# Another load order for the first units and a newly chosen order of all operations in a fused gated-linear-attention and GELU-FFN kernel

## The chip, the cores and the metric

The kernel runs on one core of one Trainium2 chip. The metric is the device time of one execution in microseconds (us); lower is better. The core has a matrix engine (TensorE; in the profile PE, its weight loads PEld), VectorE (DVE), ScalarE (ACT), GpSimd (POOL), and SyncE (SP), which here only issues transfers. Sixteen DMA engines move data between the chip's memory (HBM) and the core's working memory (SBUF); matrix products land in eight banks of PSUM.

## What is computed

The reference is a gated linear attention followed by a feed-forward block, both without biases:

```
B, H, S, D = 4, 8, 768, 48
f = sigmoid(f_logit)
for t in range(S):                       # per batch and head, state is D x D
    state = f[t][:, None] * state + outer(k[t], v[t])
    y[t]  = q[t] @ state
x = y reordered to (B*S, H*D)            # 3072 tokens x 384
h = x @ w_in                             # 384 x 2048
out = gelu_exact(h) @ w_out              # 2048 x 384
```

Inputs and the output are float32; the kernel multiplies in bfloat16 and accumulates in float32.

## The kernel before

**Tiling.** The 3072 tokens are cut into 24 chunks of 128 tokens, n = 0 to 23, and two chunks make a unit, u = 0 to 11 (chunks 2u and 2u+1; three units are one batch entry). Instead of stepping the recurrence token by token, each chunk is done with matrix products: decays are cumulated in the log domain, queries and keys are scaled by them, scores inside the chunk are masked, and a 48 x 48 state per head is carried from chunk to chunk. Each unit is also one group g of the feed-forward block.

**Names of the operations.** The names below are those in the code; a number after them is the chunk n or the unit u.

| name | engine | what it is (line) |
|---|---|---|
| fl, kt, vt, qt | SP queue | loads of logits, k, v, q of a unit: one of 384 KB for units 0 to 4 (L513), two of 192 KB from unit 5 on (L521) |
| i0, i1, i2; o0 to o3 | POOL queue | w_in in three pieces, 1024 + 512 + 512 columns (L525); w_out in four (L528) |
| E, L | ACT | exp and ln of a unit's logits (L558, L561), 0.84 us each |
| C | PE | cumulative log decays (L590, L591, L585) |
| RG, GT, GL | ACT | exp of them, both signs, and of the chunk's total (L607, L613, L634) |
| KP, QP | DVE or POOL | k and q times their decays, into tile sc (L640) |
| VC | POOL or ACT | v cast to bfloat16, into tile vb (L647) |
| Tk, Tq, then KQ | PE, then DVE or ACT | transposes of sc (L876) and their copy from PSUM (L884), units 0 to 3 |
| KD | SP queue | the same transposes done by DMA, from unit 4 on (L864) |
| A, AM | PE, DVE | scores (L1058, L995) and their masking (L901) |
| S, R, T, SB | PE, DVE, POOL, POOL | the chunk's part of the state (L1085, L1093, L1018), its addition, its decay, its copy in bfloat16 (L730, L735, L738; L925, L927, L932) |
| YI, YX, Y, YB | PE, DVE or ACT | outputs from the scores (L1113), from the state (L975), both together (L1031), and their copy (L945) |
| XT, X; XD | PE, DVE or ACT; SP queue | transposes of y (L961, L964); by DMA from unit 5 on (L949) |
| F1.g.u, GE | PE, ACT | h = x w_in in 8 parts per group (L1165, 6 matmuls, about 0.65 us) and GELU (L1175) |
| F2.n.r, O, st | PE, DVE or ACT, SP queue | out = gelu(h) w_out in four parts r per chunk, part r needing w_out piece r (L1186), its copy (L1191), its store (L1200) |

**What sets the order.** Every operation is first recorded with its engine, its reads and writes, its buffers and an assumed duration. `Plan.run` then places all of them one by one in the sequence that the list `ORDER` gives (the numbers are places in the recording order), gives each a planned start and a buffer, and the program is emitted by planned start. Each engine executes its own instructions strictly in the emitted order, so an instruction that waits holds back everything behind it on that engine. The planner's times are used for nothing else, with one exception: before a PE operation that opens a PSUM bank in the first `WARM` = 30 us, the planner fills the planned gap with multiplications of a zero tile `junk` (L1241).

**Loads.** `LOADS` fixes the order of the input transfers. On SP they are only queued, eight semaphores in turn, so the ninth load is issued when the first has landed. Where the kind of queue changes, `load` adds a wait on an earlier transfer (`gate`): i0 waits for the fourth load before it, i1 for f2, f3 for o3. The waiting instruction sits in the issuing engine's own order:

```
if order[j][0] != eng and ahead >= (AHEAD if eng == "pool" else 1.4):
    gate = late if late is not None and ahead > 5.3 and eng == "pool" else order[j][1]
```

**Tables and banks.** exp/ln and GELU are in different ACT tables, so a change between them costs a table load (L1247). The eight PSUM banks are four for F1, F2 and a few named units (`s_fh`) and four for the rest.

**Lists that choose engines.** `HVC` (units whose VC is on ACT), `HKQ` (chunks whose KQ is on ACT), `HYB`, `HX` (chunks whose YB, X is on ACT), `GKP`, `GQP` (chunks whose KP, QP is on POOL), `EG`, `ET` (units whose C or Tk/Tq use the F1 banks), `AJ` (units whose two score products are one operation).

Of the kernel before, what the change touches and what calls it, by code (L numbers as in the profile page):

```python
# [191 lines left out]
RST = []  # L192
VA = []
WIN = [1024, 512, 512]
EG = [0, 1, 4]
ET = [1]
EX = [0]
EA = [0, 1]
SPLIT = []
HVC = [1, 4]  # L200
HKQ = [0, 1, 2, 6, 8]
HYB = [1, 5]
HX = []
GKP = [2, 8]
GQP = [2, 3, 21]
GAM = []
ODVE = [0, 1, 2, 4, 6, 7, 8, 9, 10, 11, 12, 13, 14, 16, 17, 18, 19, 20, 21, 22, 23]
XDMA = [5, 6, 7, 8, 9, 10, 11]
KDMA = [4, 5, 6, 7, 8, 9, 10, 11]
AJ = [2, 4, 5, 7, 8, 10, 11]  # L210
NGT = 4
NG1 = 3
GLD = []
# [6 lines left out]
AHEAD = 4.4  # L220
UNITS = 12
WARM = 30.0
LOADS = ['f0', 'k0', 'v0', 'q0', 'v1', 'f1', 'k1', 'q1', 'i0', 'f2', 'k2', 'q2', 'v2', 'i1', 'i2', 'o0', 'o1', 'o3', 'o2', 'f3', 'f4', 'k3', 'q3', 'v4', 'q4', 'v3', 'k4', 'f5', 'k5', 'v5', 'q5', 'u6', 'u7', 'u8', 'u9', 'u10', 'u11']

PRIO = []
ORDER = [int(x) for x in """
5 6 0 21 23 22 10 26 18 9 31 20 13 12 27 28 24 7 29 14 32 33 16 15 25 11 17 121 122 123 129 8 124 30 126 130 131 132
125 135 128 34 2 3 4 133 139 136 35 39 134 140 148 127 137 141 36 138 37 38 145 192 193 194 149 152 147 146 19 150 142
151 206 195 197 196 200 201 198 144 143 202 40 41 204 205 156 157 207 210 208 158 153 211 199 203 161 209 219 212 159
160 216 220 221 162 163 223 218 42 43 213 214 265 266 164 166 170 222 215 217 44 154 155 45 47 171 228 167 229 49 230  # L230
267 224 231 232 46 234 235 168 169 233 236 239 240 243 48 50 241 244 237 242 174 245 238 165 172 247 246 173 248 225
279 227 51 53 249 52 178 251 175 250 176 273 253 179 252 177 55 272 259 180 54 56 274 277 269 271 268 270 254 186 260
276 275 283 181 187 278 57 280 284 281 291 58 59 285 292 188 282 189 226 293 295 286 190 331 255 294 332 256 60 61 182
287 288 290 289 401 62 333 339 334 183 296 184 336 335 337 402 340 261 262 341 342 300 297 343 344 347 263 346 298 301
302 299 348 403 404 405 409 63 411 412 410 64 350 349 351 1 345 338 315 305 257 352 355 65 306 66 307 309 354 356 353
414 67 68 358 408 313 359 413 316 308 406 361 362 363 360 69 314 407 317 311 303 415 258 70 310 304 318 312 357 423
417 366 424 367 325 326 370 368 371 372 327 416 467 369 425 328 426 365 468 329 71 185 72 428 429 427 475 364 379 380
373 418 383 73 74 375 381 419 422 374 384 421 420 469 377 376 378 387 476 432 388 75 436 76 264 382 77 481 430 431 78
433 79 389 319 385 437 470 471 478 477 480 472 527 80 81 82 320 434 435 473 474 528 321 438 386 479 322 323 489 390
391 482 441 442 447 443 448 451 483 444 490 445 452 453 439 491 493 535 83 446 454 440 395 484 449 450 455 485 487 84  # L240
492 601 191 85 86 486 488 529 531 530 542 396 536 494 495 496 87 539 537 497 88 89 330 461 397 392 593 456 533 534 540
594 538 541 393 498 462 551 602 604 595 607 457 543 532 597 598 596 603 605 458 557 463 398 503 544 459 606 552 399
558 600 504 90 513 514 559 553 91 561 608 499 464 545 548 505 501 599 550 616 554 560 500 547 549 610 546 617 502 507
508 618 506 562 619 511 623 609 92 93 512 555 509 521 556 563 624 510 625 522 394 94 400 324 564 95 659 667 627 515
611 620 615 613 614 660 516 523 517 518 661 662 663 668 628 96 670 664 669 97 465 612 629 519 621 575 576 98 622 672
524 525 99 577 565 579 569 578 566 665 666 671 573 681 570 580 630 682 567 571 673 100 674 675 641 568 574 683 727 626
685 643 637 572 642 101 644 631 632 102 645 635 646 638 633 676 636 634 639 653 640 103 104 105 654 684 581 680 679
734 106 677 678 107 688 686 108 647 719 655 582 720 721 728 687 689 109 723 724 730 733 722 583 526 520 460 690 725
726 729 732 785 731 648 649 587 588 650 786 656 584 736 743 787 794 651 585 744 795 797 788 735 749 750 589 590 796
791 746 745 793 751 699 790 789 591 110 111 700 740 741 737 742 701 705 754 112 702 586 113 808 693 739 738 747 706  # L250
694 691 692 799 809 755 810 800 748 697 698 695 792 798 592 114 696 707 703 756 704 657 708 709 815 710 802 801 765
769 770 711 816 757 759 760 763 115 116 117 803 771 758 766 764 806 817 118 807 805 761 772 652 658 767 752 753 812
811 859 762 804 768 851 713 820 779 773 774 813 714 821 814 119 712 852 860 862 780 853 775 861 864 822 863 855 858
854 867 856 776 715 781 782 857 783 716 866 873 835 836 717 827 874 777 819 875 818 825 823 826 828 877 120 865 876
718 824 868 872 871 870 833 831 845 829 869 832 880 881 878 837 879 834 830 846 838 847 839 784 848 840 778 882 849
841 842 889 843 890 883 897 884 893 885 894 898 886 887 895 888 891 844 850 466 899 900 896 892 901 902 905 906 903
907 908 911 912 913 909 914 904 915 910 916
""".split()]


# [1 line left out]
def kernel(  # L262
# [268 lines left out]
    def decays(u):  # L531
# [33 lines left out]
        last = 2 * u + 1 if rc[2 * u + 1] % nC == nC - 1 else None  # L565
        gps = [(s_fh if u in EG else s_m).new() for _ in range(1 if g1d else 2)]
        if g1d:
# [83 lines left out]
    def decays_hs(u):  # L651
# [3 lines left out]
        for j in range(2):  # L655
# [9 lines left out]
            def lv(j=j):  # L665
# [4 lines left out]
                  rd=[("e", n)] + z_lf, wr=[("lf", n)], bufs=[fl, lf], table="exp", prio=pr, name=f"L{n}")  # L670
            g = (s_fh if u in EG else s_m).new()

# [70 lines left out]
    def attn_hs(u):  # L743
        kq = s_kq.new()
        for c in range(2):
            n = 2 * u + c
            sc = X[n]["sc"]
            tp = (s_fh if u in ET else s_m).new()
            pr = 20 * u + 10 * c
# [107 lines left out]
    def turn(u, kq):  # L857


        for j in range(2):  # L860
            n = 2 * u + j
            sc = X[n]["sc"]
            if u in KDMA:
# [3 lines left out]
                continue  # L867
            tp = (s_fh if u in ET else s_m).new()
            pr = 20 * u + 10 * j
# [358 lines left out]

    P.run()
    PLAN.append(P)  # L1230
    state = {}
    junk = one.tile([C, 512], BF16, name="junk")
    nc.gpsimd.memset(junk, 0.0)  # L1233
    at = 0.9
    for o in P.placed:
        if o.eng == "PE":
            if o.opens is not None and o.start < WARM:
                room = int((o.start - at - 0.25) / (0.11 if o.start < 10 else 0.06))
                while room > 0:
                    w = 128 * min(room, 4)  # L1240
                    nc.tensor.matmul(o.opens.t()[:, 0:w], junk[:, 0:C], junk[:, 0:w], start=True, stop=True, skip_group_check=True)  # L1241
                    room -= 4
            at = o.end
        if o.table and state.get("t") != o.table:
            state["t"] = o.table
            if o.dur:
                nc.scalar.preload_act_table_set({"exp": "natural_log_exp_and_others", "gelu": "gelu_and_others"}[o.table])  # L1247
        o.fn()
# [32 lines left out]
```

## Time and profile before

| what | value |
|---|---|
| median of 3 runs | 181.52 us (181.39 to 181.66) |
| the profiled execution's own time | 181.36 us, of which its span is 179.6 us |
| PE busy | 170.4 us, 95% of the span, 1996 matmuls |
| ACT busy | 125.9 us (70%), 15 table loads of 1.28 us |
| DVE busy | 94.2 us (52%) |
| POOL busy | 51.9 us (29%) |
| DMA | 32.61 MB, mean 182 GB/s; reads 25.17 MB, writes 4.72 MB |
| granted PE clock | 1.00 throughout |

A line of a timeline reads: start, duration, engine, line of the program, operation, output<-input, shape, count, and in brackets how long the engine sat idle before it and what ended that idle time. A duration of a matmul is its latency; in a row of them the next starts earlier, so busy time, not the sum of durations, is what counts. The chain of waits follows the work that ended last back to its start. The window view gives the busy time of each engine in a stretch.

### The profile page before, as it was taken

Reading aid. Unit: us, or ns where it says so; the run is one execution under the profiler, and the core shown is the slowest. Engines: PE = TensorE matmul, PEld = TensorE weight load, DVE = VectorE, ACT = ScalarE, POOL = GpSimd, SP = SyncE. Lnnn points to the kernel's source line nnn. Section 1 sums busy time; section 2 is a strip of 40 time slices with the busy share of each in tenths; the row PEclk is TensorE's granted clock in tenths of the full one; section 3 lists DMA queues with packets and bytes.
Section 4 is the critical chain, followed back from the end, with each engine's and each line's share of the span. In section 5 each row is a group of like instructions: output and inputs, shape, how many; then the busy total and the mean of one; then the engine's idle time right before and its main releaser. Section 6 shows DMA issues by size and latency. Waiting matters only on the chain.

```text
span 179.6 us, 4905 instructions
## 1 busy us (share of the span) xinstructions
PE 170.4 (95%) x1996; PEld 131.6 (73%) x1998; DVE 94.2 (52%) x195; ACT 125.9 (70%) x214; POOL 51.9 (29%) x117
## 2 busy tenths in 40 slices
PE   7878899999998999999999999999999999999993
PEld 2345679866687787787689599966687976896972
DVE  6347670049887552708688681254892355471110
ACT  3768579955789999988766698677565598351620
POOL 7465684003044540122054414010431410310000
PEclk9999999999999999999999999999999999999999
DMA  6999999989999999789989998898998996932302
GB/s 149 261 261 227 264 165 191 211 199 266 230 193 206 171 232 204 153 186 218 201 159 205 214 208 173 171 182 223 154 246 98 196 241 71 183 86 47 131 0 88
DMA packets 106997, 32.61 MB, mean 182 GB/s; under 512 B 102112, under 2 KB 106080, under 8 KB 106976
## 3 DMA queue, kind: packets, MB, share of 16 engines
q1 hardware_dynamic: 105056, 29.07, 80.7%
q0 software_dynamic: 1776, 3.15, 9.9%
q8 instruction: 15, 0.25, 0.6%
q10 hardware_dynamic: 144, 0.10, 0.2%
q14 instruction: 6, 0.05, 0.1%
HBM read 25.17 MB, written 4.72 MB: 166 GB/s over the span
## 4 chain that ended last, share of the span: by engine, by line
PE 73%; ACT 12%; DVE 5%; DMA 3%; POOL 3%; issue 2%; SPq 1%; POOLq 0%; DVEq 0%; ACTq 0%
PE ps L1186 31%; PE ps L1165 29%; DMA vt<-in_v_dram 3%; ACT gT L1175 3%; DVE am L901 3%; PE ps L995 2%; ACT L1247 2%; POOL sc L640 2%; ACT kq L884 2%; PE ps L1031 2%; PE ps L1211 1%; PE ps L585 1%; ACT rg L607 1%; PE ps L876 1%; PE ps L969 1%
## 5 line engine op out<-in xcount | busy, mean ns | idle before, releaser
L1175 ACT ACTIVATE gT<-ps 128x512 bf16<-128x512 f32 x96 | 57.0, 666 | 24.2 <-PE ps L1165 23.5
L1165 PE MATMUL ps<-xT,win 128*128 128x256 bf16 x576 | 68.8, 273 | 0.8 <-ACT gT L1175 0.5
L1186 PE MATMUL ps<-wout,gT 128*128 128x384 bf16 x368 | 65.9, 326 | 0.0
L1165 PEld LDWEIGHTS <-win 128*128 128x128 bf16 x576 | 61.6, 114 | 3.4 <-issue 0.9
L1186 PEld LDWEIGHTS <-gT 128*128 128x128 bf16 x368 | 34.5, 98 | 19.6
L901 DVE TENSOR_TENSOR am<-ps,mask 128x512 bf16<-128x512 f32 x28 | 17.5, 682 | 17.9 <-PE ps L995 17.9
L927 POOL TENSOR_TENSOR tn<-rr,gl 128x384 f32<-128x384 f32 x12 | 10.3, 857 | 46.0 <-DVE rr L925 45.2
L640 DVE TENSOR_TENSOR sc<-kt,rg 128x384 bf16<-128x384 f32 x22 | 14.6, 668 | 14.4 <-ACT rg L607 14.4
L1191 DVE COPY osb<-ps 128x384 f32<-128x384 f32 x20 | 11.1, 554 | 19.3 <-PE ps L1186 19.2
L1247 ACT ACT_TABLE_LOAD x15 | 19.2, 1283 | 0.3
L647 POOL CAST vb<-vt 128x384 bf16<-128x384 f32 x20 | 10.9, 556 | 24.2 <-DMA vt<-in_v_dram 23.9
L945 DVE CAST yb<-ps 128x384 bf16<-128x384 f32 x22 | 11.5, 552 | 9.6 <-PE ps L1031 5.9
L607 ACT ACTIVATE rg<-ps 128x384 f32<-128x384 f32 x21 | 10.1, 501 | 8.0 <-PE ps L587 2.9
L640 DVE TENSOR_TENSOR sc<-qt,gt 128x384 bf16<-128x384 f32 x21 | 11.6, 558 | 6.0 <-ACT gt L613 5.8
L932 POOL CAST sb<-tn 48x192 bf16<-48x192 f32 x30 | 10.7, 361 | 13.7 <-DVE tn L921 12.6
L558 ACT ACTIVATE fl<-fl 128x768 f32<-128x768 f32 x12 | 10.2, 848 | 6.3 <-DMA fl<-in_f_logit_dram 6.3
L901 DVE TENSOR_TENSOR am<-ps,maskp 128x512 bf16<-128x512 f32 x20 | 12.6, 683 | 3.7 <-PE ps L1061 1.9
L613 ACT ACTIVATE gt<-ps 128x384 f32<-128x384 f32 x21 | 9.9, 493 | 4.0 <-PE ps L587 2.1
L561 ACT ACTIVATE lf<-fl 128x768 bf16<-128x768 f32 x12 | 10.1, 843 | 0.3
L1241 PE MATMUL ps<-junk 128*128 128x512 bf16 (+2 forms) x26 | 8.8, 475 | 1.4 <-POOL junk L1233 1.3
L925 DVE TENSOR_TENSOR rr<-ps,tn 128x384 f32<-128x384 f32 x12 | 6.6, 550 | 2.8 <-PE ps L1018 1.4
L876 PE MATMUL ps<-ident,sc 128*128 128x128 bf16 x64 | 5.1, 219 | 2.1 <-POOL ident masks.py:199 1.5
(84 smaller groups left out, 140.8 us busy)
## 6 DMA issues: line engine op xcount, KB each, us to landing
out_dram<-osb SPq DMA_DIRECT2D x19, 192.0 KB, 3.5
fl<-in_f_logit_dram SPq DMA_DIRECT2D x14, 192.0 KB, 3.9
kt<-in_k_dram SPq DMA_DIRECT2D x14, 192.0 KB, 4.0
vt<-in_v_dram SPq DMA_DIRECT2D x14, 192.0 KB, 3.9
qt<-in_q_dram SPq DMA_DIRECT2D x14, 192.0 KB, 3.9
fl<-in_f_logit_dram SPq DMA_DIRECT2D x5, 384.0 KB, 5.3
kt<-in_k_dram SPq DMA_DIRECT2D x5, 384.0 KB, 6.2
vt<-in_v_dram SPq DMA_DIRECT2D x5, 384.0 KB, 6.2
```

The lines of the kernel that those rows point to most:

```text
L607: P.add("ACT", 0.40, lambda g=gps[j], rg=rg: nc.scalar.activation(rg.t(), g.t()[:, 0:HD], AF.Exp, scale=-1.0), rd=[("g", n)], wr=[("rg", n ...
L640: P.add("POOL" if pl else "DVE", 0.80 if pl else 0.475, lambda a=a, y=y, j=j, w=w, pl=pl, b=(gtv if w else rg): (nc.gpsimd if pl else nc.v ...
L647: P.add("ACT" if hv else "POOL", 0.40 if hv else 0.47, lambda y=y, j=j, hv=hv: (nc.scalar.copy if hv else nc.gpsimd.tensor_copy)(y["vb"].t ...
L901: P.add("POOL" if pl else "DVE", 1.15 if pl else 0.61, lambda hh=hh, pl=pl: (nc.gpsimd if pl else nc.vector).tensor_tensor(ams[hh].t(), ap ...
L927: P.add("POOL", 0.83, lambda: nc.gpsimd.tensor_tensor(tn.t(), rr.t(), glb(), ALU.mult), rd=[("rr", n), ("gl", n)], wr=[("tn", n)], bufs=[r ...
L932: P.add("POOL", 0.36, lambda hh=hh: nc.gpsimd.tensor_copy(sb.t()[64 * hh:64 * hh + D, :, D * hh:D * hh + D], tn.t()[64 * hh:64 * hh + D, : ...
L945: P.add("ACT" if help_ else "DVE", 0.40 if help_ else 0.475, lambda: copier(help_)(yb.t()[:, i, :], yp.t()[:, 0:HD]), rd=[("yp", n)], wr=[ ...
L1165: nc.tensor.matmul(hps.t()[:, i * tok:(i + 1) * tok].rearrange("a (s t) -> a s t", s=s), col(fo)[:, kk, :], xT.t()[:, :, kk, :], start=(kk ...
L1175: nc.scalar.activation(to, fr, AF.Gelu)
L1186: nc.tensor.matmul(op.t()[:, 0:d_model], gT.t()[:, fo, s_ * C:(s_ + 1) * C], wout[fo // 4][:, fo % 4, :], start=(fo == 0), stop=(fo == FO ...
L1191: P.add("DVE" if od else "ACT", 0.475 if od else 0.40, lambda op=op, osb=osb, od=od: copier(not od)(osb.t(), op.t()[:, 0:d_model]), rd=[(" ...
L1247: nc.scalar.preload_act_table_set({"exp": "natural_log_exp_and_others", "gelu": "gelu_and_others"}[o.table])
```

## The change

`LOADS` is changed: f1 comes second instead of sixth, kt0 third, qt0 fourth, vt0 fifth, then qt1, kt1; i0 comes after seven loads instead of eight; vt1 comes behind i0 instead of fifth; vt2 and qt2 change places, vt3 and qt4 too, kt5 comes before fl5, and units 6 and 7 are listed load by load in the order f, k, v, q. The fourth load is now qt0, so i0 waits for qt0 and not for vt1.

`ORDER` is a new list. The lists that choose engines change as shown. Where the emission of junk multiplications looked only at whether an operation opens a bank, it now also looks whether that bank's buffer has been written before (`begun`): in the new order Tq comes before Tk for chunks 0, 2 and 3, and a junk product put ahead of such a Tk would overwrite Tq's result.

```
-EG = [0, 1, 4]
-ET = [1]
+EG = [0, 4]
+ET = [1, 4]
...
-HVC = [1, 4]
-HKQ = [0, 1, 2, 6, 8]
-HYB = [1, 5]
-HX = []
-GKP = [2, 8]
-GQP = [2, 3, 21]
+HVC = [4]
+HKQ = [1, 2, 4, 8]
+HYB = [1, 5, 22]
+HX = [0, 3]
+GKP = [2, 4, 8, 16, 23]
+GQP = [2, 3, 19, 21]
...
-AJ = [2, 4, 5, 7, 8, 10, 11]
+AJ = [2, 4, 5, 7, 10, 11]
...
-LOADS = ['f0', 'k0', 'v0', 'q0', 'v1', 'f1', 'k1', 'q1', 'i0', 'f2', 'k2', 'q2', 'v2', 'i1', 'i2', 'o0', 'o1', 'o3', 'o2', 'f3', 'f4', 'k3', 'q3', 'v4', 'q4', 'v3', 'k4', 'f5', 'k5', 'v5', 'q5', 'u6', 'u7', 'u8', 'u9', 'u10', 'u11']
+LOADS = ['f0', 'f1', 'k0', 'q0', 'v0', 'q1', 'k1', 'i0', 'v1', 'f2', 'k2', 'v2', 'q2', 'i1', 'i2', 'o0', 'o1', 'o3', 'o2', 'f3', 'f4', 'k3', 'q3', 'v4', 'v3', 'q4', 'k4', 'k5', 'f5', 'v5', 'q5', 'f6', 'k6', 'v6', 'q6', 'f7', 'k7', 'v7', 'q7', 'u8', 'u9', 'u10', 'u11']
...
-    state = {}
+    state, begun = {}, set()
...
-            if o.opens is not None and o.start < WARM:
+            if o.opens is not None and o.start < WARM and o.opens not in begun:
...
             at = o.end
+            begun.update(o.bufs)
```

What the new order does to each engine's own sequence in the first part (memsets left out; PE has 23 junk products instead of 28):

```
POOL before: trip, maskp, VC1 VC0, ident, mask, negcol, i0, SB0 SB0, KP2 QP2 QP3, T1 T2, SB.., i1 i2 o0, T3, VC5, SB3, o1 o3 o2, VC4, SB3, T4 ..
POOL after:  negcol, ident, maskp, trip, i0, VC0 VC1, QP2 QP3 KP2, SB0 SB0, T1, SB1 SB1, VC2 VC3, i1, T2, SB2 SB2, i2, mask, VC5, T3, o0 o1 o3 o2, VC4, KP4, T4 ..
ACT before:  E0 L0 RG0 RG1 GT1 GL1 GT0 KQ1 KQ0 E1 L1 VC3 RG2 GT2 RG3 GT3 VC2 GL3 YB1 KQ2 E2 L2 [gelu] 16 GE [exp] RG5 GT4 RG4 GL5 GT5 E3 L3 E4 RG6 GT6 L4 RG7 GT7 GL7 YB5 O3 KQ6 RG8 GT8 GT9 GL9 RG9 [gelu] GE2..
ACT after:   E0 L0 E1 GT0 RG1 GT1 L1 RG0 GT2 KQ1 GL3 RG3 GL1 GT3 RG2 KQ2 YB1 X0 E2 L2 [gelu] GE0.0 X3 15 GE [exp] RG4 RG5 GT4 GT5 GL5 KQ4 E3 L3 E4 L4 RG7 RG6 YB5 GT7 GL9 O3 VC9 GT6 GT8 GL7 GT9 RG8 RG9 [gelu] GE2..
DVE before:  KP0 KP1 QP1 QP0 R0 R1 AM0.1 AM0.1 AM0.0 AM0.0 KP3 YB0 KQ3 X0 R2 X1 AM1 x4 R3 YB2 YB3 X2 X3 ..
DVE after:   KP1 QP0 QP1 KP0 KQ0 AM0.0 AM0.0 AM0.1 AM0.1 KP3 R0 KQ3 YB0 R1 X1 AM1 x4 R2 R3 YB2 YB3 G5 X2 ..
PE before:   C0 C1 Tk1 Tk0 Tq1 S0 Tq0 A0.1 C2 A0.0 C3 YI0 YX1 Tk2 Tk3 Tq2 Tq3 S1 XT0 A1.1 XT1 A1.0 F1.0 x3 YI1 YX2 YX3 C4 XT2 XT3 F1 x13, F2 ..
PE after:    C0 C1 Tk1 C2 Tq0 Tq1 C3 Tk0 A0.0 Tq2 A0.1 Tq3 S0 Tk2 Tk3 YI0 YX1 A1.1 XT0 XT1 A1.0 F1.0 x2, S1, F1.0, YI1 YX2 YX3 C4 XT2 XT3 F1 x13, F2 ..
```

In the later units the sequence of each stage stays the same and single operations change places by a few positions.

## The prediction

> **What bounds the kernel now.** I read the busy tenths of the page first, then the window view, the chain of waits, and last the timelines and waits of the first 60 us engine by engine.
>
> ```profile
> PE   7878899999998999999999999999999999999993
> ```
>
> ```profile
> 21.10:34.20 13.10, 12.88 (x154) 12.14 (x154) 4.79 (x10) 11.93 (x18) 7.19 (x15) 1.00 1.09 193
> 34.20:45.00 10.80, 10.80 (x121) 6.89 (x120) 6.37 (x12) 6.73 (x12) 1.62 (x5) 1.00 1.05 229
> 45.00:54.00 9.00, 8.54 (x153) 6.78 (x153) 7.37 (x16) 7.33 (x15) 1.96 (x3) 1.00 0.96 212
> 54.00:65.40 11.40, 10.76 (x171) 8.87 (x171) 7.49 (x16) 11.30 (x17) 6.40 (x13) 1.00 1.17 199
> 65.40:90.00 24.60, 24.57 (x278) 18.75 (x278) 12.52 (x26) 22.31 (x40) 2.93 (x6) 1.00 0.99 194
> ```
>
> The columns after the stretch are length, then busy time of PE, PEld, DVE, ACT, POOL, the granted clock, DMA share, GB/s. From 21.1 us on PE is the bound: it idles 0.22 + 0 + 0.46 + 0.64 + 0.03 us here, then 0 to 130 us and 0.33 us to 176.7 us, 1.7 us in all. The last 2.9 us are the final copy and store, which stay. Products that count do not change. So the change gains only by (a) bringing the stream that begins with the first F1 forward, and (b) part of those 1.7 us; every new wait behind it costs in full.
>
> ```profile
> 1.86 5.50 DMA vt<-in_v_dram
> ...
> 15.37 3.31 POOL sc L640 x3
> ```
>
> ```profile
> 21.11 2.13 PE L1165 MATMUL ps<-xT,win 128*128 128x256 bf16 x18 [0.17 <-DVE xT L964]
> 21.00 0.85 ACT L558 ACTIVATE fl<-fl 128x768 f32<-128x768 f32 x1 [1.78 <-DMA fl<-in_f_logit_dram]
> 26.48 8.98 ACT L1175 ACTIVATE gT<-ps 128x512 bf16<-128x512 f32 x14 [1.11 <-PE ps L1165]
> 40.72 0.84 ACT L558 ACTIVATE fl<-fl 128x768 f32<-128x768 f32 x1 [2.18 <-DMA fl<-in_f_logit_dram]
> ```
>
> First two pieces of the chain (start, length), then timeline lines of PE and ACT. The lead-in goes by transfers: the trace has the eight first loads landing at 4.33, 5.85, 7.36, 8.86, 10.37, 11.88, 13.38, 14.87 us, one per 1.5 us, i0 at 20.67, fl2 at 20.97 (E2 starts then), the o pieces o0, o1, o3, o2 at 32.73, 34.47, 36.32, 38.18, and fl3, gated by o3, at 40.69 (E3).
>
> **Part 1, to the first F1.** fl1 now lands second, 5.85 instead of 11.88. After L0 (ends 6.07), E1 runs 6.1 to 6.9, GT0, RG1, GT1 at 0.41 us a step to 8.2, L1 to 9.05, RG0 9.5. Before, ACT began E1 at 12.44. DVE: KP1 7.9, QP0 8.96 (qt0 stays fourth), QP1, KP0 to 10.65 at 0.55. PE: Tq1 ends 10.5, Tk0 about 11.3. KQ1 on ACT 10.55 to 11.5, KQ0 now on DVE, 0.69 us, to 12.0; before, ACT did both one after the other (10.62 to 12.55). A0.0 at 12.1 instead of 14.6. POOL is next: vt0 lands fifth, 10.37 instead of 7.36, so VC0, VC1 end near 12.0 and QP2, QP3, KP2 (3.31 us before) run 12.0 to 15.3 instead of 15.37 to 18.68. Tk2, Tk3 end near 16.2, KQ2 and KQ3 beside each other 16.9, YI0 16.7, YX1 17.2 behind SB0, YB0/YB1 17.9, XT1 18.2, X1 18.7. xT is thus 2.4 us earlier than 21.06.
>
> win0 must be there too. Before, i0 was issued at 10.67, 0.3 after vt1's landing, its first packet moved at 14.38, its last landed 10.0 us after issue. Now it waits for qt0 (8.86): issue 9.15, landing 19.15. I take F1 at **19.1 instead of 21.1**. If the first packet has to wait for the queued loads instead, win0 stays near 20.7.
>
> **Part 2, what follows 19.1.** S1 (0.37 us) now comes after two F1. The price of vt1 behind i0: the two queues share.
>
> ```profile
> q0 software_dynamic: 252, 0.52, 90.5%
> q1 hardware_dynamic: 252, 0.10, 18.5%
> ```
>
> That is the DMA view of 15 to 18 us, with i0 in flight: packet by packet, 0.52 MB against 0.10, so an SP load gets 32 KB/us where it had 256. vt1 thereby lands at about 19.4 (as fl2 did, one load later, at 20.97). VC2, VC3 then run on POOL at 0.5 each to about 20.6, behind them i1. Two F1 end at 20.4, two junk products take 0.43, S1 starts 20.85 and F1.0.2 ends 21.85. YI1 to 22.4, YX2 22.6. YX3 wants SB2: R2 21.8, i1 stands ahead of T2 on POOL (0.8), T2 22.45, SB2 twice 0.35 to 23.15. So PE idles 0.6. C4, XT2, XT3, then F1.0.3 at 24.35. E2, L2 and the table load still end at 24.03, since fl2 is as late as before; with four banks, nothing more can be gained before that. X3 on ACT (0.39) fits between GE0.0 and GE0.1, and the 1.11 us wait of ACT at 26.48 goes. F1s end at 33.0 instead of 34.15.
>
> **Part 3, the weights.** i1 (gated by f2) goes at about 21.1 instead of 22.50, first packet 1.56 later. From there SP loads starve again: 1 KB packets of 106 ns against 26 to 30 ns give about 120 pairs per us, 47 KB/us for SP. vt2 (254 KB left) needs 5 to 6 us and lands near 28.5; before it had landed at 25.53 and o0 had been issued ahead of VC5.
>
> ```profile
> 24.08 0.58 POOL L528 DMA_DIRECT2D wout<-in_moe_w_out_dram  x1
> 25.59 0.50 POOL L647 CAST vb<-vt 128x384 bf16<-128x384 f32 x1 [0.36 <-DMA vt<-in_v_dram]
> 36.40 0.99 SPq L513 DMA_DIRECT2D fl<-in_f_logit_dram  x2
> ```
>
> Now VC5 and T3 stand before o0, o1, o3, o2 on POOL: VC5 28.6, T3 29.1, o0 29.6, first packet 31.2, landed 33.2 to 34.2 (the slowest of 16 engines came 1.0 late before). F2 begins at 33.7 (both ends: 33.2, 34.2) instead of 34.15, and o3, so fl3, comes 1.4 later: 42.1. E3, L3 end 43.85; C6, behind the same 13 F2 (8.45) and 1.8 of unit 2, is due at 44.0. It was at 44.63. So the late fl3 just fits.
>
> **Part 4, to 65 us.** L4 now runs before C6's results, KQ6 has moved to DVE, KQ4 into idle ACT time. ACT: RG7 45.55, RG6, YB5, GT7, GL9, O3 to 47.7; VC9 waits for vt4 (47.06 + 1.4 = 48.5), holding GT6 behind it; five steps of 0.41 and GL7 to 51.15, table load, GE2.0 at 52.45 instead of 54.00. PE: Tq6 waits for QP6, hence GT6, until 50.0 (0.6 idle), then two F1, A3, the fourth F1 ends 52.75. The same work ended at 53.94 before: **1.2 ahead**. Up to 65.4 ACT stays full, 1.5 ahead, PE keeps the 1.2.
>
> **Part 5, after 65 us.** Counted in PE work from rows (F1 0.654, F2 0.650), each unit keeps 8.2 us or more from its C to its A and 5.2 from Y to its F1, as before (6.9 and 5.2). Unit 5 loses most: 12.0 to 10.1; its DMA transposes landed at 78.14 for an A at 80.02, so 1.9 us of cover is used up. Unit 9, whose transposes were 0.06 us from late (129.64, A19 from 129.70), gains 1.2. GE9.7 falls behind a table change and F2.18.3 waits up to 0.3. KP4, KP16, KP23, QP19 on POOL cost 0.3 to 0.5 each under that cover. I take 0.2 lost, between 0.5 won and 1.0 lost.
>
> Sum: 1.2 - 0.2 = 1.0 off the profiled 181.36 (span 179.6 + 1.76 around it), 180.4; the median runs 0.16 above that, so **180.5**.
>
> **A rule that speaks against it.** The five junk products fewer leave PE sparser: my walk has it busy about 57% of 12 to 18.5 us. The first eleven start 427 ns apart, later ones 219; after the longest idle time since, 1.49 us at 9.76, the transposes still went at 60 ns each. By these rows nothing is lost, no gap of mine being over 0.75.
>
> The Trainium skill, "TensorE: Matmul & The Clock Gate" (Part 1, and PE-mode transpose), says that the clock halves after about 3.4 us of idling and that transposes do not count as busy. Should that catch the sparse stretch, some 3.4 us of F1 at half rate would add about 1.7 us, and the sum would be 182.2.
>
> **Rivals.** *Starved vt2 (slower).* One mechanism, on POOL: VC5 in front of o0. Each us that vt2 lands beyond 28.5 moves o0 and o3 by one; from about 29 on F2 starts later than it did. If vt2 lands at 31, F2 starts at 36.2, fl3 lands at 44.6, L3 ends 46.35, C6 is 1.7 late; ACT regains up to 0.7: 182.4 to 183.1. For it: the DMA rows above. Against it: qt2 behind vt2 isn't wanted until QP4, and a short i2 gap would let vt2 through. *Gain eaten (same).* The slowest engine makes o0 34.2 and vt4 another 0.8 later, GT6 with it: 181.3. *win0 not earlier.* F1 at 20.7, F1.0.3 at 25.5, F1s end at 34.1; only part 4 remains, 0.5: 181.0.
>
> **How the numbers follow.** About 0.2% (0.36 us) is what a measurement here tells from no change. Forecast with 0.2 to 2.0 won: 0.50, nearly all of it faster. win0 not earlier: 0.10, half faster, half same. Gain eaten: 0.10. Starved vt2: 0.27. An unseen wait after 65 us: 0.03. Faster 0.49 + 0.05 and a little of the starved case where ACT regains more: 0.56; same 0.14; slower 0.30. The range reaches from 2.0 won, 179.5, to the middle of the starved case, 182.5; the likeliest case alone has 179.5 to 181.3.
>
> **What would show it.** Right: E1 near 6.1, the first F1 near 19.1, S1 waiting for VC3, YX3 for SB2; o0 issued near 29.6 behind a VC5 that waits for vt2; fl3 landing near 42; GE2.0 near 52.5; PE as full as before after 65. Wrong: win0 landing at 20.7, o0 issued after 31, C6 after 45, an A waiting for a DMA transpose, matmuls of F1 more than 0.11 us apart before 25 us.

## The result and the profile after

The changed kernel took 180.24 us as a median (179.10 to 181.99, 8 runs) against 181.51 us before (181.39 to 182.01, 8 runs): a ratio of 0.991, 95% interval 0.9884 to 0.9935. The ratio, here and below, leaves out executions over 1.5% above their kernel's fastest, here those of 181.96 and 181.99 us. The same kernel beside the experiments took 179.26 us (ratio 0.9875, 0.9856 to 0.9894) and, on another chip, 179.42 us (0.9889, 0.9876 to 0.9901). By the medians the change saves 1.3 to 2.1 us. The profile shown is that of the repeat, an execution of 179.30 us with a span of 177.4 us. The traced execution of the first set took 181.99 us, with a later weight stream and a wait of 1.50 us at 90.87 us that the repeat has not; it is named where it differs.

The window view, with the same columns as in the prediction:

```profile
21.10:34.20 13.10, 12.54 (x178) 11.47 (x178) 2.58 (x6) 12.84 (x19) 7.29 (x16) 1.00 1.09 203
34.20:45.00 10.80, 10.72 (x130) 6.77 (x129) 5.89 (x10) 8.00 (x13) 2.82 (x6) 1.00 1.06 231
45.00:54.00 9.00, 9.00 (x162) 7.46 (x162) 8.50 (x18) 7.90 (x18) 2.27 (x3) 1.00 0.89 196
54.00:65.40 11.40, 11.40 (x172) 9.53 (x167) 7.44 (x15) 11.31 (x17) 6.04 (x13) 1.00 1.17 210
```

PE, the first number after the length, is now idle 0.56 us in the first row (0.22 before), but not at all from 45 to 65.4 us, where it had lost 0.46 + 0.64. ACT, the fourth, does 8.00 us of work between 34.2 and 45 where it did 6.73, in a stretch in which it idled: L4 (46.90 before, now 42.64) and KQ4 (from DVE) have moved there, and KQ6 (49.24 before) has left ACT for DVE.

Timelines of PE, ACT, POOL and the SP queue, the lines that answer to those shown of before:

```profile
19.22 1.50 PE L1165 MATMUL ps<-xT,win 128*128 128x256 bf16 x12 [0.55 <-DMA win<-in_moe_w_in_dram]
23.64 0.33 PE L975 MATMUL ps<-sb,kq 128*128 128x96 bf16 x4 [0.56 <-POOL sb L738]
33.56 2.76 PE L1186 MATMUL ps<-wout,gT 128*128 128x384 bf16 x16
...
25.38 9.61 ACT L1175 ACTIVATE gT<-ps 128x512 bf16<-128x512 f32 x15
40.16 0.85 ACT L558 ACTIVATE fl<-fl 128x768 f32<-128x768 f32 x1
52.08 0.77 ACT L1175 ACTIVATE gT<-ps 128x512 bf16<-128x512 f32 x1
...
24.90 0.50 POOL L647 CAST vb<-vt 128x384 bf16<-128x384 f32 x1
25.83 2.21 POOL L528 DMA_DIRECT2D wout<-in_moe_w_out_dram  x4
...
36.11 1.21 SPq L513 DMA_DIRECT2D fl<-in_f_logit_dram  x2
```

Of before, the first F2 on PE, then on ACT L4, KQ6 and GE2.0, the first GELU of unit 2:

```profile
34.15 4.06 PE L1186 MATMUL ps<-wout,gT 128*128 128x384 bf16 x24
...
46.90 0.83 ACT L561 ACTIVATE lf<-fl 128x768 bf16<-128x768 f32 x1
49.24 1.04 ACT L884 COPY kq<-ps 128x1024 bf16<-128x1024 bf16 x1
54.00 0.75 ACT L1175 ACTIVATE gT<-ps 128x512 bf16<-128x512 f32 x1
```

F1 begins 1.89 us earlier (19.22 for 21.11) and waits for win0 alone. But S1 now comes behind the first two F1, and YX3, the half-wide product of unit 1 (L975), which stood behind the first three F1 before too, waits 0.56 us for SB2. The bulk of F1 begins at 24.80 instead of 25.63 and F2 (L1186) at 33.56 instead of 34.15: of 1.89 us, 0.6 are left. The GELUs run without the 1.11 us wait, E3 (40.16) no longer waits for fl3, and GE2.0 comes at 52.08 instead of 54.00. VC5 (24.90) has no wait in its bracket: vt2 was there.

**Where the time came from.** Busy time counts the filling of PE's pipeline, so I counted matmuls: each F1 product started by a time t is worth 0.109 us and each F2 product 0.162 us, the spacing in dense stretches; the others by their own. The table is the work done beyond that of before, in us, from the traces, good to about 0.1 us (the other kernels are the experiments below):

| kernel | at 34.2 | at 54 | at 65.4 | at 90 | at 140 | at 170 |
|---|---|---|---|---|---|---|
| changed, repeat | 0.49 | 0.70 | 1.96 | 1.96 | 2.07 | 2.22 |
| changed, first set | 0.16 | 0.57 | 0.98 | -0.32 | -0.61 | -0.55 |
| changed, other chip | 0.00 | 0.65 | 1.79 | 1.64 | 1.85 | 1.90 |
| new start, old rest | 0.32 | 0.70 | 1.44 | 0.98 | 0.98 | 0.98 |
| old start, new rest | 0.00 | 0.01 | 0.11 | -0.11 | 0.43 | 0.44 |
| vt1 before i0, clock kept | -0.16 | 0.42 | 1.20 | 1.09 | 1.41 | 1.41 |
| f1 sixth, clock kept | -0.82 | -0.13 | 0.65 | 0.44 | 0.98 | 0.98 |

In the changed kernel the earlier F1 is worth 0 to 0.5 us by 34.2 us. From 34.2 to 65.4 every kernel of the table with the new order there gains another 1.1 to 1.8 us, whatever its lead-in (0.8 in the first set's execution). None of it is made before 45 us: counted in the same way at 45 us, the rows stand at 0.2, 0.2, 0.1, 0.2, 0.1 (new rest), -0.4 and -1.0. It is made where PE had lost 0.46 + 0.64 us; the rest of it would be the filling of the pipeline behind those waits, which counts as busy (not measured by itself). An earlier fl3 is not the cause: on the other chip E3 waited for fl3 until 41.36, 0.64 us later than before, and the gain from 45 to 65.4 us was as large. Around 133 us those with the new rest gain 0.1 to 0.5 (from 90 to 140 us). The first set's execution, the exception, loses 1.6 us between 65.4 and 140 us, 1.50 of it in its wait at 90.87.

### The profile page after: what moved, and what is told of

The parts are those of the page before. It is cut to its first block, busy times and chain, and to the rows that moved or that the text cites. A ratio compares the mean times of both kernels' runs of the same rounds, so it can differ in the third digit from the quotient of the medians.

```text
span 180.1 us, 4904 instructions
## 1 busy us (share of the span) xinstructions
PE 168.9 (94%) x1993; PEld 130.7 (73%) x1993; DVE 93.3 (52%) x189; ACT 126.1 (70%) x214; POOL 56.0 (31%) x123
## 4 chain that ended last, share of the span: by engine, by line
PE 62%; DMA 17%; ACT 8%; SPq 7%; DVE 2%; POOL 1%; issue 1%; DVEq 0%
PE ps L1165 28%; PE ps L1186 23%; SPq L513 7%; DMA fl<-in_f_logit_dram 6%; DMA vt<-in_v_dram 6%; ACT gT L1175 4%; DMA xT<-yb 3%; DMA kq<-sc 2%; PE ps L995 2%; PE ps L1211 1%; ACT L1248 1%; PE ps L1031 1%; ACT gt L613 1%; PE ps L969 1%; PE ps L585 1%
## 5 line engine op out<-in xcount | busy, mean ns | idle before, releaser
L1175 ACT ACTIVATE gT<-ps 128x512 bf16<-128x512 f32 x96 | 57.6, 664 | 24.7 <-PE ps L1165 23.6
L1186 PE MATMUL ps<-wout,gT 128*128 128x384 bf16 x368 | 66.0, 326 | 0.2 <-DMA wout<-in_moe_w_out_dram 0.2
L1186 PEld LDWEIGHTS <-gT 128*128 128x128 bf16 x368 | 34.3, 98 | 20.0 <-DMA wout<-in_moe_w_out_dram 0.5
L901 DVE TENSOR_TENSOR am<-ps,mask 128x512 bf16<-128x512 f32 x28 | 17.6, 683 | 21.5 <-PE ps L995 21.5
L640 DVE TENSOR_TENSOR sc<-kt,rg 128x384 bf16<-128x384 f32 x19 | 12.5, 665 | 18.4 <-ACT rg L607 18.4
L901 DVE TENSOR_TENSOR am<-ps,maskp 128x512 bf16<-128x512 f32 x20 | 12.5, 682 | 5.3 <-PE ps L1061 3.5
L640 DVE TENSOR_TENSOR sc<-qt,gt 128x384 bf16<-128x384 f32 x20 | 12.7, 642 | 3.5 <-ACT gt L613 3.0
L640 POOL TENSOR_TENSOR sc<-kt,rg 128x384 bf16<-128x384 f32 x5 | 5.0, 998 | 20.0 <-ACT rg L607 17.1
L1241 PE MATMUL ps<-junk 128*128 128x512 bf16 (+3 forms) x23 | 7.0, 428 | 1.7 <-POOL junk L1233 1.3
```

Of the source, the lines that this page charges most:

```text
L640: P.add("POOL" if pl else "DVE", 0.80 if pl else 0.475, lambda a=a, y=y, j=j, w=w, pl=pl, b=(gtv if w else rg): (nc.gpsimd if pl else nc.v ...
L901: P.add("POOL" if pl else "DVE", 1.15 if pl else 0.61, lambda hh=hh, pl=pl: (nc.gpsimd if pl else nc.vector).tensor_tensor(ams[hh].t(), ap ...
L1175: nc.scalar.activation(to, fr, AF.Gelu)
L1186: nc.tensor.matmul(op.t()[:, 0:d_model], gT.t()[:, fo, s_ * C:(s_ + 1) * C], wout[fo // 4][:, fo % 4, :], start=(fo == 0), stop=(fo == FO ...
```

## Experiments: which part of the order brings it

**New start with the old rest, and the reverse.** The changed kernel's order and loads up to about 60 us with the old order behind, and the other way round; the lists that choose engines follow their part.

```
# new start, old rest: loads up to q5, places up to 351 of ORDER are the changed kernel's
-'q5', 'f6', 'k6', 'v6', 'q6', 'f7', 'k7', 'v7', 'q7', 'u8',
+'q5', 'u6', 'u7', 'u8',
...
# old start, new rest: loads up to q5, places up to 348 of ORDER are those of before
-'f0', 'f1', 'k0', 'q0', 'v0', 'q1', 'k1', 'i0', 'v1',
+'f0', 'k0', 'v0', 'q0', 'v1', 'f1', 'k1', 'q1', 'i0',
...
```

> Load order, engine lists and order of operations of the changed kernel up to the point where unit 6's logits are queued (about 60 us), and those of the kernel before from there on. Theory (the gain is made in the first 65 us): 179.3 to 180.0, that is 1.5 to 2.2 below the kernel before, and a spread under 0.8 us, since the DMA transpose of unit 5's output (XD11) is back in its old place with 2.4 us to spare. Rival (the new order of the later units brings the gain): 181.0 to 181.7, no measurable change.

> The opposite half: everything of the kernel before up to about 60 us, load order, engine lists and order of the changed kernel after it. Theory (start): no gain, 181.2 to 183.0, with a spread of 1 us or more from the later XD11. Rival (rest): 179.6 to 180.3.

Measured: new start 180.42 us, ratio 0.9937 (0.9919 to 0.9956), by the medians 0.95 us saved, less than the 1.5 to 2.2 that I had given it; new rest 181.02 us, 0.9978 (0.9965 to 0.9991), 0.35 us saved, where I had expected none. Before stood at 181.37 us. Together that is 1.3 of 2.1 us; the new start's row falls from 1.44 at 65.4 us to 0.98 at 90, at the seam, where the joined order has waits that neither kernel has. PE lines of the new start with the old rest, then of the old start with the new rest:

```profile
66.91 0.56 PE L1113 MATMUL ps<-vb,am 64*128 64x48 bf16 x31 [0.36 <-DVE am L901]
...
132.35 0.37 PE L1031 MATMUL ps<-vb,am 128*128 128x48 bf16 x8
```

```profile
131.93 1.48 PE L1165 MATMUL ps<-xT,win 128*128 128x256 bf16 x12
133.25 0.36 PE L1031 MATMUL ps<-vb,am 128*128 128x48 bf16 x8
```

The new rest's 0.35 us is one place, unit 9. Before, PE stood idle there ahead of its second Y (L1031), which waited for the masking on DVE (am, L901): six F1 started at 132.48 and take 0.65, Y came at 133.39. With the old rest it still does (131.43, 132.35); with the new rest twelve F1 stand in front of it and there is no gap.

**The logits second, the values behind the piece.** Each of the two edits named here was undone alone. With f1 sixth, unit 1's exp, ln, sums and gates also go back behind those of unit 0 on their engines. First as it is:

```
-LOADS = ['f0', 'f1', 'k0', 'q0', 'v0', 'q1', 'k1', 'i0', 'v1', ...]
+LOADS = ['f0', 'f1', 'k0', 'q0', 'v0', 'q1', 'k1', 'v1', 'i0', ...]   # vt1 before i0
+LOADS = ['f0', 'k0', 'q0', 'v0', 'q1', 'f1', 'k1', 'i0', 'v1', ...]   # f1 sixth
```

> The changed kernel with one pair swapped: the second unit's values are loaded ahead of the first w_in piece instead of behind it (the piece's issue then waits for the load four places ahead of it, the first unit's values, which landed at 10.4 us). Everything else keeps its order. My theory, that the early first piece is what pays: the piece lands at about 20.7 us instead of 19.2, F1 begins there at about 20.8 instead of 19.22, S1 a little after the values at about 18, and most of the 1.5 us comes back as time: +0.5 to +1.0 us against the changed kernel, 179.8 to 180.3 us. Rival, that the lead-in is bounded by the third unit's logits, whose half-wide stretch of transposes (23.64 us) stands before the bulk of F1 in both: F1's first 18 matmuls are then only early work done ahead of a wait that takes their place, and the time is within 0.3 us of 179.3.

> The changed kernel with the second unit's logits back in sixth place of the loads, as before the change, and the second unit's exponential, logarithm, sums and gates moved behind the first unit's on their engines; the w_in piece still stands ahead of the second unit's values. My theory, in which the early logits pay by taking the second unit's preparation out of the way of the first unit's gates: the second unit's logits land at about 11.9 instead of 5.9 us, its transposed operands come 1 to 2 us later, F1 begins at 20 to 21 us instead of 19.22 and the time is 179.9 to 180.8 us (+0.7 to +1.5). Rival, that only the place of the w_in piece counts: F1 begins at 19.3 and the time is within 0.3 us of 179.3.

Measured: 180.27 us, ratio 0.9936 (0.9917 to 0.9955), and 181.64 us, 1.0007 (0.9989 to 1.0026), with before at 181.44. By this the logits' place was worth the whole change. But the traced executions differ in more than the order of loads. The window view and the PE timeline of the first of the two:

```profile
12.13:15.54 3.41, 2.15 (x74) 1.30 (x72) 2.28 (x5) 0.73 (x2) 3.41 (x5) 1.00 1.27 252
15.54:22.37 6.83, 6.56 (x88) 3.93 (x89) 5.17 (x11) 3.40 (x5) 3.70 (x9) 0.50 1.17 248
```

```profile
20.05 2.71 PE L1241 MATMUL ps<-junk 128*128 128x512 bf16 x7
22.59 1.47 PE L1165 MATMUL ps<-xT,win 128*128 128x256 bf16 x12
```

The granted clock (third number from the end) fell to 0.50 for 6.83 us. The seven junk products, which the planner had put into a gap that it foresaw, ran at half speed and kept PE until 22.5 us, 2 us after win0 had landed (20.50). With f1 sixth the clock was 0.50 for 3.41 us from 19.08 us on. By the mean clock of each execution this was the exception with vt1 before i0 (ten of twelve at 0.998 or more, 179.52 to 180.98 us; the traced one, 181.50, was the slowest) and the rule with f1 sixth (eleven of twelve at 0.99 or less). So both were run again with products in the gaps: fillers ahead of A0.1, itself moved into the wait (with f1 sixth ahead of C2 and S0 as well, S0 moved too), and in the first the junk ahead of F1 cut to two.

```
-room = int((o.start - at - 0.25) / (0.11 if o.start < 10 else 0.06))
+room = int((o.start - at - 0.25) / (0.11 if o.start < 10 else 0.06)) + {'A0.1': 12, 'F1.0.1': -22}.get(o.name, 0)
+# with f1 sixth: {'C2': 14, 'A0.1': 16, 'S0': 16}
```

> The second unit's values again ahead of the first w_in piece, but now with fillers placed so that TensorE's clock stays up: two 512-wide fillers and the half-wide product A0.1 put into the 0.98 us idle at 12.8 us, and the filler ahead of F1, which kept TensorE from 20.05 to 22.48 at half clock, cut to two. What the first try mixed (clock and order of loads) is thus taken apart. If the order of the loads alone costs what it seemed to: F1 at about 20.6 (the piece landed at 20.5), the third unit's half-wide product at about 24.1 instead of 23.64, granted clock 1.00 in 15 to 21 us, and 0.3 to 0.8 us more than the changed kernel. If the loss of the first try was mostly the half clock: within 0.2 us of the changed kernel. If it was the order and not the clock: 0.9 us or more.

> The second unit's logits again sixth, with TensorE kept busy: fillers in the idle stretches before the second unit's sums (2.0 us), before A0.1 and before S0 (0.6 us each). With the clock at 1.00 from 15 to 21 us the products that took 0.61 to 0.82 us in the first try take 0.40 to 0.63, F1 begins at about 20.9 instead of 21.80. If the early logits themselves are what the gain hangs on: still 1.0 to 1.8 us above the changed kernel. If the loss of the first try (some 2 us) was the half clock: under 0.6 us above it.

> The changed kernel itself, beside the three others of this group on one chip, since its median stood at 180.24 us in one set of runs and 179.26 in another. Expected: 179.2 to 180.3 us; first w_in piece landing at 19.2, F1 at 19.2, granted clock 1.00 from 6 to 24 us.

Measured on one chip, before at 181.43: the changed kernel 179.42 us (0.9889, 0.9876 to 0.9901), vt1 before i0 179.65 us (0.99, 0.9885 to 0.9914), f1 sixth 180.46 us (0.9947, 0.9935 to 0.9959). The clock was 1.00 in all three traces. PE lines of vt1 before i0, then of f1 sixth:

```profile
20.75 1.50 PE L1165 MATMUL ps<-xT,win 128*128 128x256 bf16 x12 [1.70 <-DMA win<-in_moe_w_in_dram]
...
34.29 2.93 PE L1186 MATMUL ps<-wout,gT 128*128 128x384 bf16 x17
```

```profile
21.19 1.48 PE L1165 MATMUL ps<-xT,win 128*128 128x256 bf16 x12 [0.26 <-DVE xT L964]
...
34.91 2.28 PE L1186 MATMUL ps<-wout,gT 128*128 128x384 bf16 x13
```

With vt1 ahead, F1 starts 1.4 us later than in the changed kernel beside it (20.75 for 19.36), F1 ends 0.5 later (34.29 for 33.80), F2 begins 0.2 later: S1 and YX3, which stand before the bulk of F1, give back most of it, and in the changed kernel of this group F2 waited until 34.09 for o0, which landed at 34.04. The values' place is worth 0.2 us, with intervals that overlap; with a prompt o0 it may be more. The logits' place, with the order that goes with it, is worth 1.0 us, and without it the kernel is still 1.0 us faster than before, although its F2 starts 0.8 us later: that part is the rest of the change, the order, the lists that choose engines and the other places of loads, which were not taken apart. With f1 sixth the first try took 1.2 us more (181.64 for 180.46, on two chips), and its executions sort by their mean clock: 180.83 us at 1.00, 181.33 to 181.52 at 0.99, 181.76 to 182.40 at 0.98. With vt1 before i0 the 0.6 us between the tries (180.27 for 179.65) is not the clock, which most of its executions had in full; whether it is the seven junk products or the chip was not tested.

## Experiments: the clock, the late values, and an attempt to do better

**Fewer fillers.** The rule weighed in the prediction, tried by itself:

```
-WARM = 30.0
+WARM = 8.0
```

> The changed kernel with the filler matmuls (the junk products of TensorE) given only up to 8 us instead of up to 30 us; nothing that the output needs is touched. By the rows of both traces, in which matmuls beside gaps of 0.2 to 0.6 us run at the same length as matmuls in the dense stretch (F1 pieces 0.11 us apart from the first on): no change, 179.1 to 179.5 us, with F1's first pieces still 0.11 us apart. Rival, a clock gate that closes in sparse work: F1's pieces between 19 and 25 us then come up to twice as far apart, 36 of them, up to +1.7 us, unless the wait at 23.64 us hides the first 18 (then up to +0.9). By the Trainium skill (TensorE: Matmul & The Clock Gate) the rival is the rule. A third possibility, that the fillers stand in the way of real work (0.28 us at 18.4 and 0.59 us at 20.55): up to 0.3 us faster.

Measured: 179.69 us, ratio 0.9895 (0.9875 to 0.9914), 0.3 to 0.4 us slower than the changed kernel on the other chips; the mean clock was 0.97 to 0.99 in all six executions. Window view:

```profile
6.65:10.06 3.41, 2.02 (x22) 1.05 (x20) 1.85 (x5) 3.17 (x7) 0.81 (x1) 1.00 1.28 261
10.06:20.30 10.24, 9.02 (x173) 6.38 (x174) 6.59 (x15) 4.32 (x10) 5.89 (x12) 0.50 1.19 249
```

My expectation "by the rows" was wrong: with PE busy 2.02 of 3.41 us the clock halved for 10.24 us, four transposes took 0.61 us for 0.40, and F1 began at 20.26, 1.0 us late. It cost no more because, as above, the first F1s wait later anyway: F2 began at 34.28. The clock was back as F1 began.

**The third unit's values really late.**

```
-'f2', 'k2', 'v2', 'q2', 'i1', 'i2', 'o0', ...
+'f2', 'k2', 'q2', 'i1', 'i2', 'v2', 'o0', ...
-POOL: ... i2, VC5, T3, o0, o1, o3, o2, VC4
+POOL: ... i2, T3, o0, o1, o3, o2, VC5, VC4
```

> The changed kernel with the third unit's values loaded behind the second and third w_in pieces and their two casts on GpSimd moved behind the four issues of w_out. The window of four loads then lets the second piece go when the second unit's values have landed (19.7 us) and not when the third unit's logits have (21.2 us). What I had expected of the third unit's values beside two pieces, a late landing, is made real here, but with nothing of w_out's issue behind it. Theory, that the stretch from 24 to 36 us is set by the one stream of w_in and w_out: second piece issued at about 20.8 instead of 21.44, landing at 27.0 instead of 27.8, third at 29.4 instead of 30.1, w_out's first at 31.8 instead of 32.4, and F1 and F2 move by what they waited, 0.3 to 0.6 us faster than the changed kernel (178.7 to 179.0). Rival, that the stretch is bound by TensorE from 24.8 us on and by the third unit's first products before it: no change, 179.1 to 179.5. Other side: the values land at about 27.5 and the casts end at 29, the third unit's second product waits or the gates' casts on GpSimd collide, 0.3 to 0.8 us slower.

Measured: 182.77 us, ratio 1.0037 (1.0006 to 1.0068), on the slow side and well beyond the 0.3 to 0.8 us that I gave it. I had overlooked the load's own gate: with v2 between i2 and o0, v2 waited for i1 and was issued at 25.75, and o0 waited for v2, so the casts' place did not matter. POOL, then PE:

```profile
31.43 2.21 POOL L528 DMA_DIRECT2D wout<-in_moe_w_out_dram  x4 [6.19 <-DMA vt<-in_v_dram]
```

```profile
36.25 6.41 PE L1186 MATMUL ps<-wout,gT 128*128 128x384 bf16 x28 [2.89 <-DMA wout<-in_moe_w_out_dram]
```

This is the prediction's slower rival by accident: vt2 landed at 31.14, o0 went at 31.43, F2 began at 36.25. It also brought a half clock: 0.50 for 3.41 us from 36.65 us. Its executions with a mean clock of 1.00 took 180.68 to 181.72 us (5), those at 0.99 took 182.70 to 183.67 us (7). The starved stream thus cost about 2 us by itself (181.36 us, the median at full clock, for 179.26 and 179.42 of the changed kernel on other chips), and the clock 1.9 more where it fell (183.25).

**An attempt to do better.** The second w_in piece without its wait for fl2, one cast of unit 1's values on ACT, X3 ahead of the first GELU, and no junk products in the bulk of F1:

```
-'f2', 'k2', 'v2', 'q2', 'i1', 'i2', 'o0', ...
+'f2', 'k2', 'i1', 'v2', 'q2', 'i2', 'o0', ...
-hv = u in HVC
+hv = u in HVC or n == 3
-room = int((o.start - at - 0.25) / (0.11 if o.start < 10 else 0.06))
+room = int((o.start - at - 0.25) / (0.11 if o.start < 10 else 0.06)) + {'F1.1.3': -29}.get(o.name, 0)
-ACT: E2, L2, GE0.0, X3
+ACT: E2, L2, X3, GE0.0
```

> A version meant to beat the changed kernel, on what its trace shows of 19.6 to 28 us. The second w_in piece is loaded right behind the third unit's keys, so it no longer waits for the third unit's logits (0.73 us of GpSimd idle at 20.7), one of the two casts of the second unit's values goes to ScalarE, which is idle from 18.3 to 21.2, and the copy X3 goes ahead of the first GELU. Expected if the third unit's half-wide product is what holds F1's bulk: second unit's S1 at about 20.6, that product at about 23.0 instead of 23.64, F1's bulk at 24.2 instead of 24.80, 0.3 to 0.7 us faster than the changed kernel. If the w_in and w_out stream is what holds it: within 0.2 us. On the other side: the third piece waits for the third unit's values (about 25 us), lands at 31 or later and F1 waits for it, up to 0.8 us slower.

Measured: 181.68 us, ratio 0.9995 (0.997 to 1.0019), 2.3 us slower than the changed kernel beside it. PE, then ACT:

```profile
26.91 9.69 PE L1165 MATMUL ps<-xT,win 128*128 128x256 bf16 x72 [1.95 <-ACT gT L1175]
```

```profile
24.34 0.48 ACT L964 COPY xT<-ps 128x384 bf16<-128x384 bf16 x1 [1.62 <-PE ps L961]
24.82 1.28 ACT L1248 ACT_TABLE_LOAD   x1
```

Everything up to F1's bulk came as expected (S1 20.62, YX3 22.98, F1 24.14). But X3, for which ACT waits 1.62 us, now stood ahead of the table load, which had filled that wait; the first GELU came at 26.12 instead of 24.20, F1's banks stayed full, and PE idled 1.95 us. After that gap the clock was 0.50 for 3.41 us, from 27.96 us on. Executions at a mean clock of 1.00 took 180.15 to 180.48 us (4), still 0.7 to 1.1 us above the changed kernel's 179.42; the others took 181.28 to 182.09 us (8).

**A transfer moved earlier.** The traced execution of the first set has this line on PE, which the repeat has not:

```profile
90.87 2.12 PE L1165 MATMUL ps<-xT,win 128*128 128x256 bf16 x18 [1.50 <-DMA xT<-yb]
```

```
-DVE: ... QP12, YB10 ...      SP: ... st4, XD11, KD12 ...
+DVE: ... YB10, QP12 ...      SP: ... XD11, st4, KD12 ...
```

> The changed kernel once more, unchanged, as the measure for the kernels beside it. Theory (the gain is made before 65 us, and what varies is how late a DMA transpose lands): median 179.6 to 180.5, executions spread over 1 us or more; in the profile the first w_in product at 19.2 to 19.4, GE2.0 near 52.5, and a wait at unit 5's first F1 (it was reached at 89.2) between 0 and 1.7 us long that accounts for most of the difference between executions. Rival (the spread is made in the lead-in, by the slowest DMA engine): the wait at 89 is the same in a faster execution and the first F2 is the one that moves by over 1 us.

> The changed kernel with two moves: on DVE YB10 ahead of QP12, and on the SP queue XD11 ahead of the store st4, so XD11 can be issued near 84.7 instead of 85.9. Theory (XD11 is what is late): its landing comes 1.2 us earlier, the wait at 89 to 91 us shrinks to under 0.5, median 179.0 to 179.7 and a spread under 1 us. Rival (any DMA transpose can be late, or the lead-in varies): median within 0.3 of the changed kernel beside it and the spread still over 1 us.

The two traced executions of the changed kernel are 2.7 us apart; this wait is 1.5 of it, and their first F2 differ by 0.4 (33.99 for 33.56). Measured with the two moves: 179.26 us (0.9881, 0.986 to 0.9902), the same as the changed kernel beside it (0.9875), but spread from 178.97 to 180.04 us. Neither traced execution of this pair had the wait, so it stays open whether the edit helps where the transpose is late. No version tried is faster than the changed kernel.

## Why the prediction held, point by point

**The number.** The first set's median, 180.24 us, lies 0.3 us from the 180.5 predicted; the later sets of the same kernel, 179.26 and 179.42, lie just below the range's lower end, 179.5. So the near hit is partly luck: the sizes of parts 4 and 5 were too small by about 1 us together, and late transfers, as in the first set's traced execution, took much of it away again in that set (its other executions were not traced).

**Part 1 was right in its steps.** E1 came at 6.02 (6.1 predicted), A0.0 at 12.2 (12.1), i0 was issued at 9.18 (9.15), win0 landed at 19.17 (19.15), F1 began at 19.22 (19.1). The DMA view of 13 to 16 us has i0 and the SP loads sharing packet by packet, as the rows of before had it:

```profile
q0 software_dynamic: 259, 0.53, 92.8%
q1 hardware_dynamic: 286, 0.11, 20.6%
```

**Part 2 was right in kind and 0.5 us short.** vt1 landed at 19.6 (19.4), S1 came at 21.08 (20.85), YX3 at 23.64 behind SB2 (23.15), F1's bulk at 24.80 (24.35), F1 ended at 33.56 (33.0). The gap at YX3 was named, and its size was right (0.56 us for 0.6).

**Part 3 was wrong, with the right F2.** vt2 was to land near 28.5 and o0 to go at 29.6; vt2 landed at 24.38, VC5 did not wait, o0 went at 25.83. The step that failed is "254 KB left" when i1's first packet moves. i1 was issued 0.34 us later than I took (21.44), and its packets came later after that than the 1.56 us of before: two of them up to 23.4 us, 56 in the next us. From 22.5 to 23.4 us SP still moved 0.19 MB, most of what I had left over, and from 23.4 to 24.4 us it had 411 packets to i1's 56, not one for one. Then F2 began at 33.56 (33.7 predicted), but because F1 ended there: o0 had landed at 32.38. Issued 1.75 us later than before (25.83 for 24.08), it landed 0.35 us earlier (32.73 before), so here w_out was limited by the stream behind i1 and i2 and not by its issue. fl3 landed at 39.65 (42.1) and C6 came at 44.31 (44.0).

**Part 4 was mis-sized.** GE2.0 came at 52.08 (52.45 predicted, 54.00 before). "PE keeps the 1.2" should have been 1.7 in the repeat: the second S there (L1093) goes at 56.18 for 57.87. On the other chip it goes at 56.47, 1.4 ahead, and in the first set's execution at 56.65, 1.2 ahead, as predicted. PE lines of before, then after:

```profile
54.80 0.81 PE L1165 MATMUL ps<-xT,win 128*128 128x256 bf16 x6 [0.36 <-ACT gT L1175]
...
57.87 0.51 PE L1093 MATMUL ps<-vb,sc 64*128 64x96 bf16 x16
```

```profile
54.09 2.15 PE L1165 MATMUL ps<-xT,win 128*128 128x256 bf16 x18
56.18 0.52 PE L1093 MATMUL ps<-vb,sc 64*128 64x96 bf16 x16
```

The 0.36 us wait for GELU goes, and one of 0.19 us behind it, since ACT is 1.9 us ahead there. I had left them out of the sum. I had also given the early F1 half of the gain (0.5 of 1.0 was to be left without it), and the runs show that it is the smaller part: with win0 at 20.70 and F2 at 34.29, no earlier than before, 1.8 us stay, and with the logits in their old place 1.0. That the larger part is ACT's work moved is read from the lines: L4 and KQ6 took 0.7 and 0.9 us of ACT between C6 and GE2.0 before and now take none there, 1.6 of the 1.9 us by which GE2.0 comes earlier. No run took that alone away, so it is argued and not shown.

**Part 5 had the wrong sign.** I took 0.2 us lost; the new rest alone won 0.35, at unit 9's wait for the masking on DVE. I had looked at that unit's transposes only ("0.06 us from late"), not at its second Y. And where the transfers were late, in the first set's execution, more was lost than the 1.0 I allowed: 1.6 us between 65.4 and 140, most of it one wait for the transpose of unit 5's outputs (XD11, issued at 85.93 and landed at 90.83; in the repeat 83.29 and 86.07), for which part 5 had counted on 5.2 us of work between Y and F1.

**The rule that speaks against the change** did not come true in the traces: in the repeat the clock was 1.00 from 6.3 us on, with PE busy 2.15 us or more in every 3 us up to 24. By the mean clock two of the changed kernel's 17 executions were at 0.99 (179.38 and 181.96 us). And my ground was too broad. "By these rows nothing is lost" holds for this order; with fewer fillers the clock halved in every execution, and with a 0.98 us wait in place of 0.47, in the traced execution of vt1 before i0, it did as well.

**The slower rival** named the right place. It had vt2 at 31, F2 at 36.2, 182.4 to 183.1 us; the kernel in which vt2 did land at 31.14 had F2 at 36.25 and took 182.77 us. That the time agrees is chance: at full clock that kernel took 181.36 us, a good 1 us under the rival's, whose chain of fl3 was too late (44.6 us; there 43.44), and the half clock, which I had not counted, made up for it. Half of *Gain eaten* was seen in the execution on the other chip: o0's last part landed 0.74 us behind the first 15 of 16 (34.04 for 33.30) and F2 began 0.3 us after F1's end, at 34.09; vt4 landed at 48.48, not 0.8 behind the 48.5 of part 4. That execution took 179.55 us, so a late o0 alone does not eat the gain. *win0 not earlier* was priced at 0.5 us won; with win0 at 20.70 the kernel still won 1.8.

## What to carry to other kernels

Price an early start by the next thing that all its work must pass (here the YX3 before F1's bulk), not by its own first instruction: 1.4 us of an earlier F1 were worth 0.2. Read work that leaves an engine's dense stretch for idle time ahead of it, here ACT's L4 at 34 to 45 us, as a gain of its own. And when one edit is undone to price it, look at the granted clock first, in every execution and not in the traced one alone: my price of the logits was wrong by 1.2 us until fillers held the clock, while the half clock in the trace of vt1 before i0 was missing in ten of its twelve executions.

## What the runs showed of the hardware

The granted clock of PE changed in steps of 3.41 us: 0.50 for 3.41 us (f1 sixth, the early i1, the late values), 6.83 us (vt1 before i0), 10.24 us (fewer fillers). I counted PE's busy time up to 44 us in windows of that length, set by the recorded steps, over all fourteen traces. At full clock, every window with 2.27 us or more was followed by full clock; of the nine below 2.2 us five were followed by half (0.52, 1.46, 2.03, 2.04 and 2.15 us), four were not (1.71, 1.74, 1.93 and 2.08 us). At half clock, windows with 2.62, 3.01 and 3.14 us were followed by half again, those with 3.37 us and more by full. So less busy time makes the half clock likely, not certain, and kernels at the edge spread: 180.15 to 182.09 us for the early i1, 179.15 to 179.55 for the changed kernel beside it. The kernel before is near the edge too: seven of its 61 executions beside the experiments had a mean clock of 0.991 and took 181.93 to 182.23 us, the others 180.94 to 181.64.

The Trainium skill, "TensorE: Matmul & The Clock Gate" (Part 1), has a free-running window of 3413 ns, which these steps agree with. Its section on oscillation puts the danger at idle gaps above some 3.4 us; here the longest gap in a window before a half clock was 1.18 us with fewer fillers and 0.98 us with vt1 before i0, so the measurement decides: no gap of that length is needed. The busy share of a window tells more than its longest gap, for the kernel before kept its clock after a gap of 1.49 us; between 1.7 and 2.2 us of busy time neither tells. That transposes do not count as busy, which the prediction weighed, is not borne out: with the late values the window from 12.75 us on had 0.91 us of other work, 2.29 us with the transposes, and full clock followed.
